# The first unit's output product: its second half as three products of split numbers, and a new order of the parts

## The chip, the cores and the metric

The kernel runs on one core of one Trainium2 chip. The metric is the device time of one execution in microseconds (us); the median of several runs is taken. TensorE is called PE here (PEld is its loading of weights), VectorE DVE, ScalarE ACT, GpSimd POOL, and SyncE, which issues the DMAs, SP.

## What is computed

Local attention over chunks of 32 tokens, then a channel mix ("ch" below stands for one chunk's queries and the keys and values in its reach, with 8 memory tokens):

```
a   = softmax(scale * q_ch @ k_ch.T);  x = a @ v_ch        # B=4, H=8, S=768, D=64
xk  = mu_k * x + (1 - mu_k) * x_prev;  xr = mu_r * x + (1 - mu_r) * x_prev
k   = max(xk @ w_k, 0)                                     # 512 -> 1024
v   = (k * k) @ w_v                                        # 1024 -> 512
out = sigmoid(xr @ w_r) * v
```

The weights arrive as 64-bit floats and become fp32 on the chip; the result is fp32.

## The kernel before

**Units.** The 4 x 768 tokens are cut into 12 units of 256 tokens (`UTOK`), each of two blocks of 128 tokens (c = 0, 1). Each unit goes through scores (named s in the order below), transposes of the softmax (t, one for each block), the product with v (a, one for each block, giving x), the hidden layer (h, four parts, each with 256 of the 1024 hidden columns), the gate (g, one for each block), and the output product (v, or p from unit 2 on).

**Two ways to multiply.** An fp32 product takes fp32 operands as they are. The split way writes each number as a high part and a low part of the type fp32r (`kh`, `kl` for the squared activations, `wv_hl` for w_v, `xh`, `xl` for the mixed inputs) and makes three products in place of one: high x high, high x low, low x high. Unit 0 is done in fp32 all through (`is_whole`, line 383), unit 1 by split products, and units from `FAST` = 2 on by a scheme of seven split products (`products`, line 743).

**The output product of units 0 and 1** (lines 1099 to 1157). For each block c there are two parts of the inner sum over 1024: half 0 uses the hidden columns of f = 0 and 1, half 1 those of f = 2 and 3. So its parts are named v0.0.0 (unit 0, block 0, half 0), v0.0.1, v0.1.0 and v0.1.1. Both halves of a block accumulate in one bank of PSUM (`pv`). In unit 0 a part is four fp32 products of 128 x 512 (line 1112), each of which stands in the trace as two records; in unit 1 it is twelve split products (line 1124). When a block's two parts are done, DVE multiplies with the sigmoid of the gate (`f_o`, line 1145) and SP stores it.

**Preparing the operands.** ACT applies relu and square to the hidden layer (lines 1047, 1054); for split products ACT or DVE then writes `kh` (line 1060) and DVE `kl` (line 1072). Each of the ten weight pieces (four of w_k, two of w_r, four of w_v) is loaded as 64-bit words, joined to fp32 on ACT and DVE (lines 325 to 332), and later split: the high part by ACT or DVE (line 335, shown under the copying helper, lines 271 and 273), the low part by DVE (line 345). The low parts of w_v go to buffers in which raw pieces of w_v lay (`lows`, line 300), two pieces to a buffer. For units after the first, the mixed input is made by a difference (`df`, line 607), a mixing (line 617), a high part and a low part (`xl`, line 633).

**Storage order.** The columns of w_v and w_r are put by the host into two halves (even columns first). Split products read the moving operand "woven" (`woven`, line 50: one word from each half in turn), which puts the result back into natural order. Unit 0's fp32 products read it straight, and the final multiply undoes the order (line 1149).

**What sets the order.** Every operation is given to a planner (`Plan`, line 81) with a cost, the operations that it waits for, and its buffers. PE's order is written out by hand for the start (`LEAD`, line 34) and continued by `te_order` (line 186); the first 230 planned operations (`STRICT`) keep PE strictly in that order. Operations of the other engines have no order of their own: each gets a due time, counted back from those that need it, and the planner gives every engine the operation that can start first, with a preference for the earlier due time (line 166). Each engine, and SP's queue of DMAs, then runs its list strictly in turn.

Of the kernel before, what the change touches and what calls it, by code (L numbers as in the profile page):

```python
# [16 lines left out]
P = 128  # L17
# [3 lines left out]
DM, DFF = 512, 1024  # L21
# [3 lines left out]
KT = DM // P  # L25
# [2 lines left out]
NEG = -3.0e38  # L28
TINY = 2.0**-112
LOOK = 400  # L30
STRICT = 230
EASE = 0.1
TURNS = 3
LEAD = "s0.0 s0.1 t0 a0 t1 a1 h0.0.0 h0.0.1 s1.0 h0.1.0 h0.2.0 s1.1 h0.3.0 h0.3.1 h0.3.2 h0.3.3 g0.0 g0.1 t2 t3 v0.0.0 a2 a3 v0.0.1 s2.0 v0.1.0 v0.1.1 h1.0 h1.1 t4 t5 h1.2 a4 a5 h1.3 g1.0 g1.1"
UTOK = 256
FAST = 2
ROWS = [(0, 0, 1), (0, 1, 1), (1, 0, 2), (2, 0, 2), (3, 0, 2)]
# [19 lines left out]
def pairs(a):  # L57
    return a.rearrange("p (n t) -> p n t", t=2)
# [127 lines left out]
def te_order():  # L186

    nu = B * S // UTOK
    seq = [tuple([x[0]] + [int(n) for n in x[1:].split(".")]) for x in LEAD.split()]
    for u in range(1, nu):  # L190
        a, b = 2 * u + 2, 2 * u + 3
        g = [("g", u + 1, c) for c in range(QPU)]
        h = [("h", u, f) for f in range(FT // 2)]
        v = [("v", u, c, n) for c in range(QPU) for n in range(2)]
        n = 1 if u == nu - 2 else 2
        seq += h[:n] + [("t", a), ("t", b)] + h[n : n + 1] + [("a", a), ("a", b)] + h[n + 1 :]
        if u >= FAST:
            v = [("p", u, n) for n in (1, 7, 6, 4, 5, 2, 3)]
            if u >= nu - 2:
                g = [("g", nu - 1, u - (nu - 2))]  # L200
            if u == nu - 1:
                v = v[:5] + [("p", u, 2, 0), ("p", u, 3), ("p", u, 2, 1)]
            seq += v[:2] + [("s", u + 2, 0)] + g + v[2:]
            continue
        seq += v[:1] + [("s", u + 2, 0)] + g + v[1:]
    seq = list(dict.fromkeys(seq))
    last = {"t": B * NQT, "a": B * NQT}
    seq = [x for x in seq if x[1] < last.get(x[0], nu)]
    due, t = {}, 6.0
    for x in seq:  # L210
        assert x not in due
        due[x] = t
        t += PE_COST[x[0]] * (0.66 if x[:3] == ("h", 0, 0) else 0.33 if x[:3] == ("h", 0, KT - 1) else 1.32 if x[:2] == ("h", 0) else 1.32 if x[1] == 0 and x[0] in "gv" else 1)
    return due


# [1 line left out]
def local_attention__then__channel_mix(  # L218
# [56 lines left out]
    def either(late=False, **alts):  # L275
        return [(n, *alts[n]) for n in alts if n != "pool"]
# [103 lines left out]
    def word_deps(hl, ks):  # L380
        return [whole[id(hl[0]), k][0] for k in ks], [whole[id(hl[0]), k][1] for k in ks]

    def is_whole(u, part):
        return u == 0

    xdone = {}
    xslot, pslot = {}, {}
# [547 lines left out]
    def channel_mix(u):  # L935
        b, t0 = units[u]

        def f_gate(c):
            p = T["pr", u, c] = ps("m", f"pr{u}_{c}")
            if is_whole(u, "g"):  # L940
                for k in range(KT):
                    w = T["w", id(wr_hl[0]), k // 2][:, k % 2 * DM : (k % 2 + 1) * DM]
                    nc.tensor.matmul(  # L943
                        p, T["xf", u, 1][:, k, c * P : (c + 1) * P], w, start=(k == 0), stop=(k == KT - 1)
                    )
                return
            xh, xl = T["xh", u, 1], T["xl", u, 1]
            wh, wl = ([w[k // 2][:, k % 2 * DM : (k % 2 + 1) * DM] for k in range(KT)] for w in wr_hl)
            for k in range(KT):
                for n, (x, w) in enumerate(((xh, wh[k]), (xh, wl[k]), (xl, wh[k]))):  # L950
                    nc.tensor.matmul(  # L951
                        pairs(p), x[:, k, c * P : (c + 1) * P], woven(w),
                        start=(k + n == 0), stop=(k == KT - 1 and n == 2),
                    )

        def f_sig(c):
            if c == 0:
                T["sg", u] = sb("sg", [P, QPU * DM], f"sg{u}")
            p, sg = T["pr", u, c], T["sg", u][:, c * DM : (c + 1) * DM]
            if is_whole(u, "v") and not is_whole(u, "g"):  # L960
                p = p.rearrange("p (n t) -> p t n", t=2)
                sg = sg.rearrange("p (t n) -> p t n", t=2)
            nc.scalar.activation(sg, p, AF.Sigmoid)  # L963

        wr, wr_use = wdeps(wr_hl, range(KT // 2)), []
        if is_whole(u, "g"):
            wr, wr_use = word_deps(wr_hl, range(KT // 2))
        sgs = Slot("sg")
        gs = [Slot("m") for _ in range(QPU)]
# [1 line left out]
        for c in range(QPU):  # L971
            grp.append(
                op(
                    ("pe", FULL if is_whole(u, "g") else BLOCK), lambda c=c: f_gate(c),
                    grp[-1:] + (list(mix[u, 1][0].values()) if is_whole(u, "g") else list(mix[u, 1][:2])) + wr,
                    new=[gs[c]], use=list(mix[u, 1][2:]) + wr_use, due=due["g", u, c],
                )
            )
# [41 lines left out]
        for f in range(FT // 2):  # L1020
# [39 lines left out]
                copy(e, h, part())  # L1060

            kl = Slot("st") if f == 0 else Slot("kh4") if f == 1 else Slot("kf0") if f == 2 else kl

            def f_lo(e, f=f, part=part, kl=kl):
                if f < 2:
                    l = sb(kl.tag, [P, 2, UTOK], f"kl{u}_{f}", F32R)
                else:
                    if f == 2:
                        T["kl", u] = sb(kl.tag, [P, 4, UTOK], f"kl{u}_{f}", F32R)
                    l = T["kl", u][:, 2 * f - 4 : 2 * f - 2]  # L1070
                T["kl", u, f] = l
                e.tensor_sub(l, part(), T["kh", u, f].bitcast(F32))
# [10 lines left out]
            )  # L1083
            relu = oa
            ob = op(either(act=(0.54,), dve=(0.62, True)), f_sq, [oa], use=[kf])
            if is_whole(u, "v") or u >= FAST:
                ks.append((ob, None, kf, kf))
                continue
            o2 = op(either(act=(0.54,), dve=(0.35, True)), f_hi, [ob], new=[kh], use=[kf])
            o3 = op(  # L1090
                either(dve=(0.62, True)), f_lo, [o2] + ([o3] if f == 3 else []),
                new=[kl] * (f < 3), use=[kf, kh] + [kl] * (f == 3),
            )
            ks.append((o2, o3, kh, kl))

# [3 lines left out]
        for c in range(QPU):  # L1099
            s = Slot("m")  # L1100
            prev = None
            for half in range(2):
                fs = range(FT // 4 * half, FT // 4 * (half + 1))

                def f_s2(c=c, half=half, fs=fs):
                    if half == 0:
                        T["pv", u, c] = ps("m", f"pv{u}_{c}")
                    p = T["pv", u, c]
                    if is_whole(u, "v"):
                        for f in [2 * f2 + i for f2 in fs for i in range(2)]:  # L1110
                            w = T["w", id(wv_hl[0]), f // 2][:, f % 2 * DM : (f % 2 + 1) * DM]
                            nc.tensor.matmul(  # L1112
                                p, T["kf", u, f // 4][:, f % 4, c * P : (c + 1) * P], w, start=(f == 0), stop=(f == FT - 1)
                            )
                        return
                    wh, wl = ([w[f // 2][:, f % 2 * DM : (f % 2 + 1) * DM] for f in range(FT)] for w in wv_hl)
                    for f2 in fs:
                        for i in range(2):
                            f = 2 * f2 + i
                            kh = T["kh", u, f2][:, i]  # L1120
                            kl = T["kl", u, f2][:, i]
                            tc_ = slice(c * P, (c + 1) * P)
                            for n, (x, w) in enumerate(((kh, wh[f]), (kh, wl[f]), (kl, wh[f]))):
                                nc.tensor.matmul(  # L1124
                                    pairs(p), x[:, tc_], woven(w), start=(f + n == 0), stop=(f == FT - 1 and n == 2)
                                )

                deps, use = [prev], []
                for f in fs:
                    deps += ks[f][:2]  # L1130
                    use += ks[f][2:]
                if is_whole(u, "v"):
                    wd, wd_use = word_deps(wv_hl, fs)
                    deps += wd
                    use += wd_use
                else:
                    deps += wdeps(wv_hl, fs)
                dv = due["v", u, c, half]
                prev = op(("pe", FULL if is_whole(u, "v") else BLOCK), f_s2, deps, new=[s] if half == 0 else [], use=use + ([s] if half else []), due=dv)
                if u == 0:  # L1140
                    first_v.append(prev)
                if u == FAST - 1:
                    last_v.append(prev)

            def f_o(c=c):
                o = T["o", u, c] = sb("o", [P, DM], f"o{u}_{c}")
                p, sg = T["pv", u, c], T["sg", u][:, c * DM : (c + 1) * DM]
                if is_whole(u, "v"):
                    o, p, sg = pairs(o), woven(p), woven(sg)
                nc.vector.tensor_mul(o, p, sg)  # L1150

            def f_st(c=c):
# [81 lines left out]
```

## Time and profile before

| | us |
|---|---|
| Median of 3 runs | 389.33 (388.58 to 390.25) |
| The profiled execution | 389.12 |
| Its span in the profile | 387.3 |
| PE busy | 381.1 (98%) |
| DVE busy | 317.7 (82%) |
| ACT busy | 219.6 (57%) |
| Output product of unit 0, line 1112 (32 records) | 14.4 busy |
| Output product of unit 1, line 1124 (48 records) | 18.3 busy |

The granted clock of PE is 1.0 throughout. The span runs from the first to the last instruction on the chip; the profiled execution's own time has some 2 us more around it. A group of PE instructions shows each record's time from its start to its modelled end; neighbours overlap, so the time that a stage takes on PE is read from the chain or from the starts in the timeline. In a line of the timeline stand start, duration, engine, line, operation, output and inputs, the shapes, and how many such instructions were merged.

### The profile page before, as it was taken

How to read it: one execution, taken by the hardware profiler on the slowest of the kernel's cores; microseconds unless marked ns; L12 is line 12 of the kernel's file. 1: busy time of each engine (PE TensorE's matmuls, PEld its weight loads, DVE VectorE, ACT ScalarE, POOL GpSimd, SP SyncE). 2: the span in 40 equal slices, each digit the busy share in tenths (PEclk: the TensorE clock that was granted, in tenths of full speed). 3: DMA queues.
4: the chain of work that ended last, by engine and by line, in shares of the span. 5: the costliest groups of instructions: out<-in, count | busy, mean ns of one | idle time of the engine just before them, and what ended most of it. 6: DMA issues, size and time to landing. Idle time of an engine off the chain costs nothing.

```text
span 387.3 us, 10714 instructions
## 1 busy us (share of the span) xinstructions
PE 381.1 (98%) x4768; PEld 350.8 (91%) x4768; DVE 317.7 (82%) x509; ACT 219.6 (57%) x326; POOL 2.8 (1%) x13
## 2 busy tenths in 40 slices
PE   8899999999999999999999999999999999999996
PEld 6786559988999999999999999999999999999996
DVE  2998999998799699699699689789779869969264
ACT  1797985763645564464465366267267356567260
POOL 2000000000000000000000000000000000000000
PEclk9999999999999999999999999999999999999999
DMA  8999882320052143134134134134134120000101
GB/s 313 418 397 396 312 287 89 110 83 27 30 193 84 52 155 121 54 122 155 54 113 164 57 110 164 56 110 164 56 110 164 57 90 22 30 29 2 54 2 54
DMA packets 13053, 48.98 MB, mean 126 GB/s; under 512 B 1488, under 2 KB 1872, under 8 KB 12496
## 3 DMA queue, kind: packets, MB, share of 16 engines
q1 hardware_dynamic: 13008, 48.31, 33.4%
q8 instruction: 37, 0.61, 0.7%
q14 instruction: 8, 0.07, 0.1%
HBM read 42.01 MB, written 6.29 MB: 125 GB/s over the span
## 4 chain that ended last, share of the span: by engine, by line
PE 97%; DVE 1%; issue 0%; ACT 0%; DVEq 0%
PE ph L1028 31%; PE pr L951 15%; PE accy L856 10%; PE accz L856 7%; PE accx L856 7%; PE px L526 6%; PE s L429 4%; PE ph L1000 4%; PE pv L1112 4%; PE pt L509 3%; PE pv L1124 3%; PE pr L943 2%; PE warm L1180 2%; DVE mx L442 0%; DVE e L447 0%
## 5 line engine op out<-in xcount | busy, mean ns | idle before, releaser
L1028 PE MATMUL ph<-xh,wk 128*128 128x256 f32 x352 | 99.0, 281 | 0.0
L1028 PE MATMUL ph<-xl,wk 128*128 128x256 f32 x352 | 96.8, 275 | 0.0
L1028 PE MATMUL ph<-xh,wl 128*128 128x256 f32 x352 | 96.8, 275 | 0.0
L1047 ACT ACTIVATE kf<-ph 128x512 f32<-128x512 f32 x47 | 27.9, 598 | 73.8 <-PE ph L1028 73.7
L1028 PEld LDWEIGHTS ph<-xh,wk 128*128 128x128 f32 x352 | 67.5, 192 | 0.9 <-issue 0.2
L1028 PEld LDWEIGHTS ph<-xl,wk 128*128 128x128 f32 x352 | 67.6, 192 | 0.3 <-issue 0.2
L1028 PEld LDWEIGHTS ph<-xh,wl 128*128 128x128 f32 x352 | 67.6, 192 | 0.0
L273 DVE COPY aTz<-pt 64x512 f32<-64x512 f32 x20 | 13.9, 694 | 27.5 <-PE pt L509 18.0
L951 PE MATMUL pr<-wr,xh 128*128 128x512 f32 x88 | 34.3, 390 | 0.0
L801 DVE TENSOR_TENSOR al<-kf,ah 128x512 fp32r<-128x512 f32 x50 | 33.5, 686 | 0.5
L951 PE MATMUL pr<-wr,xl 128*128 128x512 f32 x88 | 33.4, 379 | 0.0
L951 PE MATMUL pr<-wl,xh 128*128 128x512 f32 x88 | 33.4, 379 | 0.0
L453 ACT ACTIVATE e<-e 128x1024 f32<-128x1024 f32 (+1 forms) x13 | 12.9, 992 | 34.7 <-DVE e L447 34.6
L526 PEld LDWEIGHTS px<-aTz,vw 128*64 128x64 f32 x768 | 23.5, 138 | 3.8 <-issue 1.8
L526 PE MATMUL px<-aTz,vw 128*64 128x64 f32 x768 | 25.2, 224 | 1.1 <-issue 1.1
L1054 ACT ACTIVATE kf<-kf 128x512 f32<-128x512 f32 x40 | 25.3, 633 | 1.3 <-DVE kf L1049 0.4
L271 ACT CAST ah<-kf 128x512 fp32r<-128x512 f32 x40 | 24.9, 622 | 1.8 <-DVE kf L779 1.2
L271 ACT CAST xh<-df 128x1024 fp32r<-128x1024 f32 x11 | 16.3, 1482 | 12.2 <-DVE df L617 12.2
L856 PE MATMUL accx<-wl,ah 128*128 128x256 f32 x80 | 22.0, 275 | 0.0
L856 PE MATMUL accx<-wv,al 128*128 128x256 f32 x80 | 22.0, 275 | 0.0
L856 PE MATMUL accx<-wv,ah 128*128 128x256 f32 x80 | 22.0, 275 | 0.0
L963 ACT ACTIVATE sg<-pr 128x512 f32<-128x512 f32 x24 | 14.3, 604 | 10.3 <-PE pr L951 10.3
(124 smaller groups left out, 937.2 us busy)
## 6 DMA issues: line engine op xcount, KB each, us to landing
qk<-in_qk_dram SPq DMA_DIRECT2D x24, 768.0 KB, 6.2
vw<-in_vw_dram SPq DMA_DIRECT2D x24, 512.0 KB, 4.6
out_dram<-o SPq DMA_DIRECT2D x23, 256.0 KB, 2.0
raw<-in_w_k_dram SPq DMA_DIRECT2D x4, 1024.0 KB, 12.5
raw<-in_w_v_dram SPq DMA_DIRECT2D x4, 1024.0 KB, 9.4
raw<-in_w_r_dram SPq DMA_DIRECT2D x2, 1024.0 KB, 8.0
out_dram<-o SPq DMA_DIRECT2D x2, 128.0 KB, 1.7
id_sb<-in_ident_dram SPq DMA_DIRECT2D x1, 64.0 KB, 5.5
```

The source lines that it names most:

```text
L271: e.copy(dst, src)
L429: nc.tensor.matmul(s5[CHUNK * j : CHUNK * (j + 1), h, d - c, r, :], q4[z, r, j, :], k4[z, r, j, :], start=True, stop=True,)
L526: nc.tensor.matmul(p3[64 * h : 64 * h + 64, 2 * g : 2 * g + 2, CHUNK * j : CHUNK * j + CHUNK], v[:, g, h, j, :], a[:, h, g, j, :], start=True,
L801: nc.vector.tensor_sub(low(n), place[n](), T["ah", u, n].bitcast(F32))
L856: nc.tensor.matmul(o, x, w, start=(n in fresh and c + i == 0), stop=(c == cs[-1] and i == 2), skip_group_check=True)
L951: nc.tensor.matmul(pairs(p), x[:, k, c * P : (c + 1) * P], woven(w), start=(k + n == 0), stop=(k == KT - 1 and n == 2),)
L963: nc.scalar.activation(sg, p, AF.Sigmoid)
L1000: nc.tensor.matmul(p[:, i * UTOK + c * P : i * UTOK + (c + n) * P], T["w", id(wk_hl[0]), k][:, fc], T["xf", u, 0][:, k, z], start=(i + k + ...
L1028: nc.tensor.matmul(pairs(p[:, i * UTOK : (i + 1) * UTOK]), w[:, fc], x[:, :, k].rearrange("p t n -> p n t"), start=(k + n == 0), stop=(k = ...
L1047: e.activation(part(), p, AF.Relu)
L1054: e.activation(q, q, AF.Square)
L1112: nc.tensor.matmul(p, T["kf", u, f // 4][:, f % 4, c * P : (c + 1) * P], w, start=(f == 0), stop=(f == FT - 1))
```

## The change

1. `is_whole` takes the half of the inner sum: unit 0's gate and hidden layer and half 0 of its output product stay fp32; half 1 (v0.0.1 and v0.1.1) is made by three split products, for which `kh` and `kl` of f = 2 and 3 are made for unit 0 too, and pieces 2 and 3 of w_v must be split by then.
2. So that both halves fit in one bank of PSUM, the fp32 products of gate and output read w woven, too; the sigmoid and the final multiply no longer reorder.
3. `kl` of unit 0 gets buffers of its own (`sl`, `sm6`), which the seven-product scheme uses later.
4. The hand-written order: v0.1.0 comes before v0.0.1; t4, t5, a4 and a5 come after all of h1.0 to h1.3 (t4 and t5 ahead of g1.0, a4 and a5 between g1.0 and g1.1); v1.0.0 and s3.0 are now part of the list. `STRICT` goes to 260. The due times count v's half 1 as a split product.

```diff
-STRICT = 230
+STRICT = 260
-LEAD = "... g0.0 g0.1 t2 t3 v0.0.0 a2 a3 v0.0.1 s2.0 v0.1.0 v0.1.1 h1.0 h1.1 t4 t5 h1.2 a4 a5 h1.3 g1.0 g1.1"
+LEAD = "... g0.0 g0.1 t2 t3 v0.0.0 a2 a3 v0.1.0 s2.0 v0.0.1 v0.1.1 h1.0 h1.1 h1.2 h1.3 t4 t5 g1.0 a4 a5 g1.1 v1.0.0 s3.0"
...
-    def is_whole(u, part):
-        return u == 0
+    def is_whole(u, half=0):
+        return u == 0 and half == 0
...
                     nc.tensor.matmul(
-                        p, T["xf", u, 1][:, k, c * P : (c + 1) * P], w, start=(k == 0), stop=(k == KT - 1)
+                        pairs(p), T["xf", u, 1][:, k, c * P : (c + 1) * P], woven(w),
+                        start=(k == 0), stop=(k == KT - 1),
                     )
...
             kl = Slot("st") if f == 0 else Slot("kh4") if f == 1 else Slot("kf0") if f == 2 else kl
+            if u == 0:
+                kl = Slot(("sl", "sm6")[f % 2])
...
-            if is_whole(u, "v") or u >= FAST:
+            if is_whole(u, z) or u >= FAST:
                 ks.append((ob, None, kf, kf))
                 continue
...
-                    if is_whole(u, "v"):
+                    if is_whole(u, half):
...
                             nc.tensor.matmul(
-                                p, T["kf", u, f // 4][:, f % 4, c * P : (c + 1) * P], w, start=(f == 0), stop=(f == FT - 1)
+                                pairs(p), T["kf", u, f // 4][:, f % 4, c * P : (c + 1) * P], woven(w),
+                                start=(f == 0), stop=False,
                             )
...
-                if is_whole(u, "v"):
-                    o, p, sg = pairs(o), woven(p), woven(sg)
                 nc.vector.tensor_mul(o, p, sg)
```

More of the change, by code (lines that the diff above doesn't have):

```diff
@@ L30 @@
 LOOK = 400
-STRICT = 230
+STRICT = 260
 EASE = 0.1
 TURNS = 3
-LEAD = "s0.0 s0.1 t0 a0 t1 a1 h0.0.0 h0.0.1 s1.0 h0.1.0 h0.2.0 s1.1 h0.3.0 h0.3.1 h0.3.2 h0.3.3 g0.0 g0.1 t2 t3 v0.0.0 a2 a3 v0.0.1 s2.0 v0.1.0 v0.1.1 h1.0 h1.1 t4 t5 h1.2 a4 a5 h1.3 g1.0 g1.1"
+LEAD = "s0.0 s0.1 t0 a0 t1 a1 h0.0.0 h0.0.1 s1.0 h0.1.0 h0.2.0 s1.1 h0.3.0 h0.3.1 h0.3.2 h0.3.3 g0.0 g0.1 t2 t3 v0.0.0 a2 a3 v0.1.0 s2.0 v0.0.1 v0.1.1 h1.0 h1.1 h1.2 h1.3 t4 t5 g1.0 a4 a5 g1.1 v1.0.0 s3.0"
 UTOK = 256
@@ L212, in te_order @@
         due[x] = t
-        t += PE_COST[x[0]] * (0.66 if x[:3] == ("h", 0, 0) else 0.33 if x[:3] == ("h", 0, KT - 1) else 1.32 if x[:2] == ("h", 0) else 1.32 if x[1] == 0 and x[0] in "gv" else 1)
+        t += PE_COST[x[0]] * (0.66 if x[:3] == ("h", 0, 0) else 0.33 if x[:3] == ("h", 0, KT - 1) else 1.32 if x[:2] == ("h", 0) else 1.32 if x[1] == 0 and x[0] in "gv" and (x[0], x[-1]) != ("v", 1) else 1)
     return due
@@ L939, in f_gate @@
             p = T["pr", u, c] = ps("m", f"pr{u}_{c}")
-            if is_whole(u, "g"):
+            if is_whole(u):
                 for k in range(KT):
@@ L959, in f_sig @@
             p, sg = T["pr", u, c], T["sg", u][:, c * DM : (c + 1) * DM]
-            if is_whole(u, "v") and not is_whole(u, "g"):
-                p = p.rearrange("p (n t) -> p t n", t=2)
-                sg = sg.rearrange("p (t n) -> p t n", t=2)
             nc.scalar.activation(sg, p, AF.Sigmoid)
         wr, wr_use = wdeps(wr_hl, range(KT // 2)), []
-        if is_whole(u, "g"):
+        if is_whole(u):
             wr, wr_use = word_deps(wr_hl, range(KT // 2))
@@ L973, in channel_mix @@
                 op(
-                    ("pe", FULL if is_whole(u, "g") else BLOCK), lambda c=c: f_gate(c),
-                    grp[-1:] + (list(mix[u, 1][0].values()) if is_whole(u, "g") else list(mix[u, 1][:2])) + wr,
+                    ("pe", FULL if is_whole(u) else BLOCK), lambda c=c: f_gate(c),
+                    grp[-1:] + (list(mix[u, 1][0].values()) if is_whole(u) else list(mix[u, 1][:2])) + wr,
                     new=[gs[c]], use=list(mix[u, 1][2:]) + wr_use, due=due["g", u, c],
@@ L1062, in channel_mix @@
             kl = Slot("st") if f == 0 else Slot("kh4") if f == 1 else Slot("kf0") if f == 2 else kl
+            if u == 0:
+                kl = Slot(("sl", "sm6")[f % 2])
             def f_lo(e, f=f, part=part, kl=kl):
-                if f < 2:
+                if f < 2 or u == 0:
                     l = sb(kl.tag, [P, 2, UTOK], f"kl{u}_{f}", F32R)
@@ L1090, in channel_mix @@
             o3 = op(
-                either(dve=(0.62, True)), f_lo, [o2] + ([o3] if f == 3 else []),
-                new=[kl] * (f < 3), use=[kf, kh] + [kl] * (f == 3),
+                either(dve=(0.62, True)), f_lo, [o2] + ([o3] if f == 3 and u else []),
+                new=[kl] * (f < 3 or u == 0), use=[kf, kh] + [kl] * (f == 3 and u > 0),
             )
@@ L1112, in f_s2 @@
                             nc.tensor.matmul(
-                                p, T["kf", u, f // 4][:, f % 4, c * P : (c + 1) * P], w, start=(f == 0), stop=(f == FT - 1)
+                                pairs(p), T["kf", u, f // 4][:, f % 4, c * P : (c + 1) * P], woven(w),
+                                start=(f == 0), stop=False,
                             )
                         return
-                    wh, wl = ([w[f // 2][:, f % 2 * DM : (f % 2 + 1) * DM] for f in range(FT)] for w in wv_hl)
                     for f2 in fs:
@@ L1119, in f_s2 @@
                             f = 2 * f2 + i
+                            wh, wl = (w[f2][:, i * DM : (i + 1) * DM] for w in wv_hl)
                             kh = T["kh", u, f2][:, i]
@@ L1122, in f_s2 @@
                             tc_ = slice(c * P, (c + 1) * P)
-                            for n, (x, w) in enumerate(((kh, wh[f]), (kh, wl[f]), (kl, wh[f]))):
+                            for n, (x, w) in enumerate(((kh, wh), (kh, wl), (kl, wh))):
                                 nc.tensor.matmul(
@@ L1131, in channel_mix @@
                     use += ks[f][2:]
-                if is_whole(u, "v"):
+                if is_whole(u, half):
                     wd, wd_use = word_deps(wv_hl, fs)
@@ L1138, in channel_mix @@
                 dv = due["v", u, c, half]
-                prev = op(("pe", FULL if is_whole(u, "v") else BLOCK), f_s2, deps, new=[s] if half == 0 else [], use=use + ([s] if half else []), due=dv)
+                prev = op(("pe", FULL if is_whole(u, half) else BLOCK), f_s2, deps, new=[s] if half == 0 else [], use=use + ([s] if half else []), due=dv)
                 if u == 0:
@@ L1147, in f_o @@
                 p, sg = T["pv", u, c], T["sg", u][:, c * DM : (c + 1) * DM]
-                if is_whole(u, "v"):
-                    o, p, sg = pairs(o), woven(p), woven(sg)
                 nc.vector.tensor_mul(o, p, sg)
```

## The prediction, made before the result was known

> **What bounds the kernel now.** I read the page first: its span, the busy shares and the engines of the chain that ended last; then who kept PE (TensorE) waiting.
>
> ```profile
> span 387.3 us, 10714 instructions
> PE 381.1 (98%) x4768; PEld 350.8 (91%) x4768; DVE 317.7 (82%) x509; ACT 219.6 (57%) x326; POOL 2.8 (1%) x13
> PE 97%; DVE 1%; issue 0%; ACT 0%; DVEq 0%
> ```
>
> ```profile
> PE warm L1180 <- DVE zero_sb L260: 1.2, 1, 1.2
> PE px L526 <- issue: 1.1, 2, 0.6
> ```
>
> PE is busy for 98% of the span, the chain lies on it for 97%, and its longest waits (1.2 us at the very start, 1.1 us in two pieces) are over before the stage that the change touches. So the kernel is bound by what is issued to PE. Time leaves it when PE's list gets shorter, and comes back as soon as PE has to wait. The busy column of PE alone wouldn't prove this, since matmul ends are modelled; the chain does, where one piece starts when the piece before it ends. I therefore read the chain in order of time, from the first product with w_v on (start us, us, what):
>
> ```profile
> 41.78 3.44 PE pv L1112 x8
> ...
> 47.23 3.63 PE pv L1112 x8
> ...
> 52.28 7.06 PE pv L1112 x16
> 59.34 5.36 PE ph L1028 x48
> 64.70 0.87 PE pt L509 x8
> ...
> 68.25 2.02 PE px L526 x64
> ...
> 73.14 5.18 PE pr L951 x24
> 78.32 2.59 PE pv L1124 x12
> 80.91 1.41 PE s L429 x89
> 82.33 5.38 PE pr L951 x24
> ```
>
> The first unit's output parts are 41.78 (v0.0.0), 47.23 (v0.0.1) and 52.28 (v0.1.0 and v0.1.1 together), in fp32. Unit 1 does the same sum by split products (L1124). 52.28 + 7.06 = 59.34, so there is no hole ahead of h1.0; and so on to 82.33. To this belong the instructions by form:
>
> ```profile
> L1112 PE MATMUL pv<-w,kf 128*128 128x512 f32 x32 | 14.4, 599 | 0.0
> ...
> L1124 PE MATMUL pv<-wv,kh 128*128 128x512 f32 x16 | 6.1, 379 | 0.0
> ```
>
> **What PE saves.** One part (one 128-token block, half of the inner sum) has four blocks of the sum. The fp32 form shows two records for each, 8 a part: 3.44 us, or 0.43 us a record. (The 599 ns of the group is an instruction from start to modelled end; the ends overlap, so it is not what PE pays.) The split form has three products for each block, 12 a part: 2.59 us, 0.216 us each. The change turns two parts (v0.0.1, v0.1.1) from the first form into the second: 2 x 3.44 - 2 x 2.59 = 1.70 us less on PE. The 0.19 us by which the second part (3.63) exceeds the first follows the small matmuls that stand ahead of it; 82.33 shows the same 0.2 behind the scores for split products (5.38 against 5.18), so it stays, wherever the parts are put.
>
> The load of weights is the one thing here that could spoil this:
>
> ```profile
> L1112 PEld LDWEIGHTS pv<-w,kf 128*128 128x128 f32 x32 | 5.8, 190 | 6.4 <-issue 6.2
> ...
> L1124 PEld LDWEIGHTS pv<-wv,kh 128*128 128x128 f32 x16 | 3.0, 189 | 0.4
> ```
>
> ```profile
> 78.16 0.38 PE L1124 MATMUL pv<-wv,kh 128*128 128x512 f32 x1
> 78.38 0.38 PE L1124 MATMUL pv<-wl,kh 128*128 128x512 f32 x1
> ```
>
> Loads go from 8 to 12 a part, at 189 ns each. The products start 0.22 us apart although a load of 0.19 us lies between them, so the load runs beside the product before it. The Trainium skill (TensorE: Matmul & The Clock Gate, Part 3, What overlaps and what doesn't) says that a load overlaps running matmuls only when it targets another row group. These loads use all 128 rows, so by that rule they would not overlap; the trace, with 0.22 us from start to start, does not agree.
>
> **The form of the remaining fp32 products.** The gate of unit 0 (16 records) and its remaining fp32 halves (16) now read their moving operand "woven", alternating between the two halves of the row, and write in order; the trace has no fp32 product of that kind. The nearest row is L1124, which reads woven words of the same four bytes at 0.216 us for 512, twice as fast as an fp32 record. A reader that delivers that rate is not the limit of a record that takes 0.43 us. I take zero. The bounds: each record takes twice as long (32 x 0.43 = +13.8 us), or they come down to 0.216 us (-6.8 us). The sigmoid and the final multiply move as many elements as before: zero.
>
> **What the other engines get.** The low and high halves of w_v and of the squared activations are now wanted at v0.0.1, not first at unit 1. Rows of DVE around that time, then one of ACT:
>
> ```profile
> 45.08 1.23 DVE L332 SCALAR_TENSOR_TENSOR w<-w,raw 128x1024 uint32<-128x1024 uint32 x1
> 46.22 2.48 DVE L345 TENSOR_TENSOR wl<-w,wk 128x1024 fp32r<-128x1024 f32 x2
> 48.61 1.22 DVE L607 TENSOR_TENSOR df<-xT 128x1024 f32<-128x1024 f32 x1
> 49.87 1.67 DVE L617 SCALAR_TENSOR_TENSOR xf<-df,mu_sb,xT 128x256 f32<-128x256 f32 x4
> 51.57 0.70 DVE L1150 TENSOR_TENSOR o<-pv,sg 128x512 f32<-128x512 f32 x1
> 52.19 1.22 DVE L345 TENSOR_TENSOR wl<-w,wk 128x1024 fp32r<-128x1024 f32 x1
> ...
> 53.64 1.23 DVE L442 TENSOR_REDUCE mx<-s 128x16 f32<-128x1024 f32 x1
> 54.78 1.22 DVE L633 TENSOR_TENSOR xl<-xf,xh 128x1024 fp32r<-128x1024 f32 x1
> 55.91 1.22 DVE L447 TENSOR_TENSOR e<-s,mx 128x1024 f32<-128x1024 f32 x1
> ...
> 64.20 1.22 DVE L345 TENSOR_TENSOR wl<-w,wr 128x1024 fp32r<-128x1024 f32 x1
> ...
> 68.25 0.69 DVE L1072 TENSOR_TENSOR kl<-kf,kh 128x512 fp32r<-128x512 f32 x1
> 68.85 1.22 DVE L345 TENSOR_TENSOR wl<-w,wv 128x1024 fp32r<-128x1024 f32 x1
> ...
> 76.91 1.67 DVE L617 SCALAR_TENSOR_TENSOR df<-df,mu_sb,xT 128x256 f32<-128x256 f32 x4
> ...
> 79.28 1.23 DVE L633 TENSOR_TENSOR xl<-xf,xh 128x1024 fp32r<-128x1024 f32 x1
> ```
>
> ```profile
> 48.98 2.00 ACT L271 CAST wv<-w 128x1024 fp32r<-128x1024 f32 x2
> ...
> 63.35 0.64 ACT L271 CAST kh<-kf 128x512 fp32r<-128x512 f32 x1
> ```
>
> DVE starts its next instruction 0.1 us before the record of the last one ends: a subtraction of 1024 costs it 1.14 (54.78 to 55.91), one of 512 0.60 (68.25 to 68.85). Two kl are new (1.2 us); two wl of w_v move forward from after 67 us to before 52 us (2.28 us). DVE thus has 3.48 us more to do ahead of unit 1, and no hole to put it in; PE meanwhile arrives 1.70 us earlier. I go through PE's deadlines, carrying the order of DVE of before along:
>
> *v0.0.1, now at 52.28* (v0.1.0 has taken its place ahead of the scores). The join of the last w_v piece ends by 46.2 (both wl wait for it: their tile reuses its load buffer). Two wl and two kl behind it end at 46.2 + 3.48 = 49.7. One wk subtraction may still stand ahead of them: 50.8. ACT must put the casts of pieces 2 and 3 of w_v (1.0 us each) where it casts others at 48.98, and add two kh (0.64 each) once the squares are there. Cost zero, 1.5 us of cover; without that cover each instruction more ahead of it would cost 1.14.
>
> *h1.0, at 59.34 - 1.70 = 57.64.* It needs xl, which ended at 54.78 + 1.22 = 56.0. With 3.48 more ahead of it, less the 0.62 of the output multiply of 51.57 (its part now ends only near 55), it would end at 58.9: 1.2 us of stall. But the maximum of the scores at 53.64 (with its memset about 1.25 us) need not stand ahead of it. The planner ranks by due time, counted back from the first reader on PE, and t4 moves behind all four h1 parts, from 64.70 to 57.64 + 4 x 2.68 = 68.36 (5.36 for two parts). So xl falls due first and ends at 57.6. Stall between 0 and 1.2; I take 0.2, since the rank favours xl.
>
> *g1.0, at 68.36 + 0.87 = 69.23.* The last it needs is the second wl of w_r, which ended at 64.20 + 1.22 = 65.4; plus 3.48 gives 68.9. Zero, with 0.3 us of cover. The transposes t4 and t5 need the softmax that stood ahead of that row, and come no earlier than 68.36.
>
> *g2.0.* PE runs g1.0, a4 and a5, g1.1, v1.0.0 and the scores from 69.23 (2.59 + 2.02 + 2.59 + 0.2 + 2.59 + 1.41): 80.63, where it was 82.33. It needs the xl that ended at 79.28 + 1.23 = 80.5. The two wl are done either way before it, so only the 1.2 of the kl is added: 81.7; less the mixing of the other operand at 76.91 (1.6), due only at h2.0: 80.1. Its input chain starts later too: a5 ends at 73.84, and a copy to xT (about 0.6 as an estimate from the 512-wide rows), one df (1.14), one mix (1.6), a cast (0.7, as an estimate from the kl row) and xl (1.14) end at 79.0. Cover 0.5 us; I take zero.
>
> **What moves on the queues.** The output multiply and store of block 0 come some 4 us later. On SP's queue the next two loads of q and k stand behind that store, and the loads of vw for t6 and t7 wait for the later a4 and a5:
>
> ```profile
> 52.74 1.95 SPq L404 DMA_DIRECT2D qk<-in_qk_dram  x2
> ...
> 69.37 1.26 SPq L503 DMA_DIRECT2D vw<-in_vw_dram  x2
> ```
>
> Even 4 us later the first are issued more than 20 us ahead of the scores that follow v1.0.0, and the second come 3 to 4 us later, with unit 2 still to start. POOL has nothing in this stage. Zero.
>
> **The sum.** The profiled execution took 389.12 us: 387.3 of span and 1.8 around it. 389.12 - 1.70 + 0.2 = 387.6. The median of the three runs (389.33) lies 0.2 above the profiled one, so on that scale I say 387.8 us.
>
> **Rivals.**
>
> *DVE piles up ahead of h1.0 (20%).* If DVE keeps the maximum and the subtraction of the scores (53.64 and 55.91, 1.25 + 1.14) ahead of xl, as it is free to do once v0.0.1 is served, xl ends at 57.6 + 2.4 = 60.0 and h1.0 stalls by 2.4: slower by 0.7, 390.0 us. Should the multiply be kept in front as well (0.6), it is 390.6. It decides from the point where the stall at h1.0 passes 1.70 us. For it: DVE has no hole. Against it: the due times, and that xl is ready for it.
>
> ```profile
> 52.30:59.30 7.00, 7.00 (x18) 3.17 (x19) 6.88 (x10) 5.23 (x6) 0.00 (x0) 1.00 0.81 290
> ```
>
> Here (PE, PEld, DVE, ACT, POOL, then the granted clock) DVE is busy 6.88 of 7.00 us, ACT 5.23. The clock of PE is 1.00, as there is no hole. The Trainium skill (TensorE: Matmul & The Clock Gate, Part 1) states that an idle window of about 3.4 us halves that clock; no run shown here has such a hole, and 2.4 us would be shorter.
>
> *The gain is lost in small waits further on (6%).* g1.0 and g2.0 have 0.3 and 0.5 us of cover. If each misses by one 1024-wide instruction (1.14), the waits are 0.8 and 0.6; with the 0.2, gain is 0.1: 389.2.
>
> *The woven fp32 products run at another rate (5%).* +13.8 - 1.7 would be 401.4, -6.8 - 1.7 would be 380.8. For either speaks only that no row shows them.
>
> *Loads do not hide (2%).* Then a record of a part costs its stream and its load: 16 x (0.43 + 0.19) against 24 x (0.216 + 0.189), 9.9 against 9.7: a gain of 0.2, 389.1. The starts at 78.16 and 78.38 speak against it.
>
> **How the numbers follow.** My forecast, stalls from 0 to 0.8 us and so a gain of 0.9 to 1.7, has 67%: 387.6 to 388.4. The range must leave out no more than 2 in 10: below, the full 1.70 and the spread of a median (the three runs span 388.58 to 390.25) take it to 386.8; above, the first rival takes it to 390.1. A difference of 0.5%, about 1.95 us, is what a measurement of this kernel can tell from no change; the full saving on PE (1.70 us, 0.44%) is just below it. So faster by over 0.5% comes from the forecast only when no stall at all meets a favourable measurement (three tenths of it, 0.20) and from the faster half of the woven case (0.02) and chance order on DVE and ACT elsewhere (0.02): 0.24. Slower by over 0.5% needs a stall over 3.6 us, a quarter of the first rival (0.05), and the slower half of the woven case (0.03): 0.08. The rest, 0.68, is no change that can be told.
>
> **What would show it.** Right: pv L1112 falls to 16 records, two split parts of 2.59 us appear behind s2.0, h1.0 starts at 57.6 to 57.9, g1.0 near 69.3, g2.0 near 80.7, from there on each piece of PE's chain is 1.5 us earlier, and the gate still takes 6.9 us for 16 records. Wrong on the stall: PE idle ahead of h1.0 with xl or wl of w_k as releaser (first rival), or ahead of g1.0 or g2.0 (second). Wrong on the rate: a gate record far from 0.43. It would also be wrong if waits of PE beyond 125 us, where the change touches nothing, came or went.

## The result, and the profile after

The changed kernel takes 390.95 us (median of 7 runs, 390.65 to 391.51), the kernel before 388.85 (median of 7): a ratio of 1.005, 95% interval 1.0035 to 1.0066. That is slower by 2.1 us by the medians (1.4 to 2.6 by the interval), where a gain of 1.5 was forecast, and above the stated range of 386.8 to 390.1. The page of the profile after, first the span and the busy shares, then who kept PE waiting:

```profile
span 388.5 us, 10736 instructions
...
PE 382.2 (98%) x4776; PEld 351.8 (91%) x4776; DVE 319.1 (82%) x510; ACT 221.4 (57%) x329; POOL 2.8 (1%) x13
```

```profile
PE warm L1179 <- DVE zero_sb L260: 1.2, 1, 1.2
PE px L526 <- issue: 1.1, 2, 0.6
PE s L429 <- issue: 0.3, 1, 0.3
PE pt L509 <- DVE e L463: 0.2, 1, 0.2
```

No new wait of PE: the kernel before has the same four waits, of the same length. The 2.1 us are therefore in PE's own list, and the chain in order of time (start us, us, what) shows in which piece:

```profile
17.21 3.78 PE ph L998 x32
...
33.32 8.64 PE pr L943 x16
...
42.83 4.32 PE pv L1112 x8
...
49.16 4.51 PE pv L1112 x8
...
55.09 5.38 PE pv L1125 x24
60.47 10.72 PE ph L1026 x96
...
72.06 2.59 PE pr L952 x12
...
83.45 5.38 PE pr L952 x24
...
96.60 5.36 PE ph L1026 x48
```

The same chain of the kernel before, where it wasn't shown yet:

```profile
17.94 3.77 PE ph L1000 x32
...
34.04 6.87 PE pr L943 x16
...
95.47 5.36 PE ph L1028 x48
```

The gate of unit 0, still fp32 with 16 records, went from 6.87 to 8.64 us; a first half of 8 records from 3.44 to 4.32. Both are 0.540 us a record in place of 0.430. The two split parts (55.09) take 5.38, as forecast. The start-up of a profiled execution varies by up to 1 us (the first hidden product starts between 17.14 and 18.11 in the profiles of all runs here), so stages are best compared from the first hidden product to h2.0: 95.47 - 17.94 = 77.53 before, 96.60 - 17.21 = 79.39 after, +1.86. The parts add up: 32 records x 0.110 = +3.53, less the 1.70 saved, = +1.83. From h2.0 to the end both have the same left, 387.3 - 95.47 = 291.8 and 388.5 - 96.60 = 291.9. In the groups by form, kernel after and then kernel before, the slower record shows too, in the mean:

```profile
L1112 PE MATMUL pv<-w,kf 128*128 128x512 f32 x16 | 9.1, 709 | 0.0
L943 PE MATMUL pr<-w,xf 128*128 128x512 f32 x16 | 8.8, 703 | 0.0
```

```profile
L943 PE MATMUL pr<-w,xf 128*128 128x512 f32 x16 | 7.0, 592 | 0.0
```

599 and 592 ns became 709 and 703: 0.11 us for each record, in the gate and in the output product alike.

### The profile page after: what moved, and what is told of

It is laid out like the page before. It is cut to its first block, busy times and chain, and to the rows that moved or that the text cites. A ratio compares the mean times of both kernels' runs of the same rounds, so it can differ in the third digit from the quotient of the medians.

```text
span 388.5 us, 10736 instructions
## 1 busy us (share of the span) xinstructions
PE 382.2 (98%) x4776; PEld 351.8 (91%) x4776; DVE 319.1 (82%) x510; ACT 221.4 (57%) x329; POOL 2.8 (1%) x13
## 4 chain that ended last, share of the span: by engine, by line
PE 97%; DVE 1%; issue 0%; ACT 0%; DVEq 0%
PE ph L1026 31%; PE pr L952 15%; PE accy L856 10%; PE accz L856 7%; PE accx L856 7%; PE px L526 6%; PE s L429 4%; PE pv L1125 4%; PE ph L998 4%; PE pt L509 3%; PE pv L1112 2%; PE pr L943 2%; PE warm L1179 1%; DVE mx L442 0%; DVE e L447 0%
## 5 line engine op out<-in xcount | busy, mean ns | idle before, releaser
L273 DVE COPY aTz<-pt 64x512 f32<-64x512 f32 x20 | 13.8, 692 | 28.3 <-PE pt L509 19.1
```

## The experiments

My theory after the result (W): reading the moving operand woven costs an fp32 record a quarter of its time. Rivals: the order or the write in PSUM (P), other traffic at that time (T), the new order of the parts (O).

**Straight read, spread write.** The changed kernel, with the weave moved from the read to the write:

```diff
-pairs(p), T["xf", u, 1][:, k, c * P : (c + 1) * P], woven(w),
+p.rearrange("p (n t) -> p t n", t=2), T["xf", u, 1][:, k, c * P : (c + 1) * P], w.rearrange("p (t n) -> p t n", t=2),
...
-pairs(p), T["kf", u, f // 4][:, f % 4, c * P : (c + 1) * P], woven(w),
+p.rearrange("p (n t) -> p t n", t=2), T["kf", u, f // 4][:, f % 4, c * P : (c + 1) * P], w.rearrange("p (t n) -> p t n", t=2),
```

> The changed kernel, but unit 0's fp32 products (16 records of the gate, 16 of the first halves) read w straight and write the result spread over the bank (every second word), so the order in PSUM stays natural. Theory W (reading the moving operand woven costs an fp32 record 0.11 us, 0.54 in place of 0.43): both groups return to 0.43 us a record, PE's list is 32 x 0.11 = 3.5 us shorter, and the time falls from 391.0 to about 387.4. Rival P (it is the order of the columns in PSUM, or the write, that costs): stays at 0.54 and 391.0, or comes out slower still. Rival T (other traffic in 33 to 54 us slows PE there): stays at 0.54. For the stalls on DVE: with h1.0 some 3.5 us earlier, near 57, xl (which ended at 57.9 in the changed kernel) may now be late; 0 to 1.2 us of waiting there.

387.68 us against 388.92 of the kernel before, ratio 0.9967 (0.9954 to 0.998). The chain:

```profile
17.20 3.77 PE ph L998 x32
...
33.30 6.87 PE pr L943 x16
...
41.04 3.44 PE pv L1112 x8
...
46.49 3.63 PE pv L1112 x8
...
51.53 5.38 PE pv L1125 x24
56.91 10.72 PE ph L1026 x96
67.62 0.87 PE pt L509 x8
68.50 2.59 PE pr L952 x12
...
93.04 5.36 PE ph L1026 x48
```

Both groups are back at 0.43; T falls, and so does P: the columns lie in PSUM in the same order as in the changed kernel, and the write is now the spread one. From 17.20 to 93.04 are 75.84 us, 1.69 less than before: the saving on PE in full. The medians of the whole time differ by 1.24 us, 0.8 to 1.8 by the interval of the ratio. It beats both kernels. This run also tests the forecast of DVE's deadlines, as h1.0 comes as early as it was reckoned. From DVE's timeline:

```profile
54.61 1.53 DVE L633 TENSOR_TENSOR xl<-xf,xh 128x1024 fp32r<-128x1024 f32 x1
...
58.70 1.23 DVE L442 TENSOR_REDUCE mx<-s 128x16 f32<-128x1024 f32 x1
...
67.84 1.22 DVE L345 TENSOR_TENSOR wl<-w,wr 128x1024 fp32r<-128x1024 f32 x1
...
78.26 1.23 DVE L633 TENSOR_TENSOR xl<-xf,xh 128x1024 fp32r<-128x1024 f32 x1
```

xl ends at 56.1, ahead of h1.0 (56.91), and the maximum of the scores stands behind it, not in front. The second low half of w_r ends at 69.1, 0.6 after the start of g1.0, and costs nothing: it belongs to the second half of the inner sum, which g1.0 reaches 1.3 us after its start.

**Everything of unit 0 straight,** its 24 split products too:

```diff
-pairs(p), T["xf", u, 1][:, k, c * P : (c + 1) * P], woven(w),
+p, T["xf", u, 1][:, k, c * P : (c + 1) * P], w,
...
-pairs(p), T["kf", u, f // 4][:, f % 4, c * P : (c + 1) * P], woven(w),
+p, T["kf", u, f // 4][:, f % 4, c * P : (c + 1) * P], w,
...
-pairs(p), x[:, tc_], woven(w), start=(f + n == 0), stop=(f == FT - 1 and n == 2)
+pairs(p) if u else p, x[:, tc_], woven(w) if u else w,
+start=(f + n == 0), stop=(f == FT - 1 and n == 2)
...
+if u == 0:
+    o, p, sg = pairs(o), woven(p), woven(sg)
 nc.vector.tensor_mul(o, p, sg)
```

> The changed kernel, but everything of unit 0 that reads w_v or w_r reads it straight, the 24 split products of its second halves too; the final multiply undoes the order as in the kernel before. Theory W: the fp32 records return to 0.43 us. For the 24 split products the two theories differ: if the weave costs only fp32 and does nothing for fp32r, they stay at 0.216 us and the time is that of the first kernel, about 387.4; if fp32r is the type that gains from the weave (as every split product in the kernel uses it), straight ones take longer, say 0.27 to 0.43 us, and 1.3 to 5 us of the saving goes.

388.06 us, ratio 0.9975 (0.9966 to 0.9984). The fp32 groups are at 6.87 and 3.44 us again, but

```profile
52.14 5.80 PE pv L1125 x24
```

the split products take 0.42 us more than woven (5.38). Without the 0.2 us at the start that is 0.233 us each against 0.216. So fp32r gains from the weave by which fp32 loses, but by less than expected (0.27 to 0.43 us straight, 1.3 to 5 us in all).

**The woven gate alone,** put into the kernel before:

```diff
-p, T["xf", u, 1][:, k, c * P : (c + 1) * P], w, start=(k == 0), stop=(k == KT - 1)
+pairs(p), T["xf", u, 1][:, k, c * P : (c + 1) * P], woven(w), start=(k == 0), stop=(k == KT - 1)
...
-o, p, sg = pairs(o), woven(p), woven(sg)
+o, p, sg = pairs(o), woven(p), pairs(sg)
```

> The kernel before with one part of the change alone: unit 0's gate reads w_r woven (16 records); its output product stays fp32 and straight. Theory W: the gate takes 8.6 us in place of 6.9, the output product stays at 0.43 us a record, the time rises by 1.8 us, to 390.6 with the kernel before at 388.9. Rivals P and T: T says no change at all (order and traffic are those of the kernel before), P the same as W.

391.07 us, ratio 1.005 (1.0037 to 1.0063), 1.9 us by the ratio. The gate alone went up, by 1.77 us, and the output product, still straight, did not. The order of the parts, the split products and the write (in order, one word beside the next) are as in the kernel before here, so the read alone is left as the cause:

```profile
33.24 8.64 PE pr L943 x16
...
42.75 3.43 PE pv L1112 x8
```

**The new order alone,** in the kernel before: only `LEAD` and `STRICT`.

```diff
-STRICT = 230
+STRICT = 260
-LEAD = "... v0.0.0 a2 a3 v0.0.1 s2.0 v0.1.0 v0.1.1 h1.0 h1.1 t4 t5 h1.2 a4 a5 h1.3 g1.0 g1.1"
+LEAD = "... v0.0.0 a2 a3 v0.1.0 s2.0 v0.0.1 v0.1.1 h1.0 h1.1 h1.2 h1.3 t4 t5 g1.0 a4 a5 g1.1 v1.0.0 s3.0"
```

> The kernel before with the new hand-written order and STRICT = 260 alone; all arithmetic as before. If the order is free (theory W): within 0.3 us of the kernel before, 388.9, no waits of PE. Rival O (the order costs, through DVE or the later transposes): slower by 1 to 3 us, with PE waiting ahead of g1.0 or g2.0.

388.8 us, ratio 0.9999 (0.999 to 1.0008); 77.53 us from the first hidden product (18.10) to h2.0 (95.63), as before. O falls: the order by itself is free, to within the 0.4 us of the interval.

**The weave on other fp32 products.** The first experiment, with unit 0's hidden layer reading its mixed input woven where it has 256 columns:

```diff
+weave = woven if n == 2 else lambda a: a
...
-p[:, i * UTOK + c * P : i * UTOK + (c + n) * P], T["w", id(wk_hl[0]), k][:, fc],
-T["xf", u, 0][:, k, z],
+weave(p[:, i * UTOK + c * P : i * UTOK + (c + n) * P]), T["w", id(wk_hl[0]), k][:, fc],
+weave(T["xf", u, 0][:, k, z]),
```

> The first run (straight read, spread write for gate and first halves), and besides unit 0's hidden layer with 256 columns (48 fp32 records) reads the mixed input woven over 128 words and writes spread, so the result is in its place. A dose of the weave on other fp32 products: if it costs a quarter of the record, 0.222 becomes 0.28 and the 10.75 us of these 48 records become 13.4, the kernel 2.7 us slower than the first run (about 390.4); if the cost is 0.11 us a record whatever its width, 5.3 us; if it needs rows of 512 or w as operand, nothing.

The pieces with 256 columns, in the first experiment and then in this run:

```profile
21.75 7.10 PE ph L998 x32
...
29.65 3.65 PE ph L998 x16
```

```profile
22.66 8.94 PE ph L999 x32
...
32.39 4.56 PE ph L999 x16
```

7.10 + 3.65 = 10.75 us became 13.50: +2.75, 0.057 for 256 columns where 512 cost 0.110. So the cost goes with the columns and is not special to w. The write is spread here too, which cost nothing at 512 columns in the first experiment. One run took 390.75, with the kernel before at 389.07.

**Which orders of reading are slow?** Five runs with other orders, the gate and the first halves in fp32, the two split parts in fp32r, each 512 words with the write contiguous; they leave out putting the columns of unit 0's output back in place. In place of `woven(w)` stands, in the changed kernel, one of these (with `m`, `s` and `n` as named):

```diff
-woven(w)
+w.rearrange("p (t n m) -> p n t m", t=2, m=2)
+w.rearrange("p (n s) -> p s n", s=2)
+w.rearrange("p (b e n) -> p b n e", e=2, n=32)
```

The first reads pairs (quads with m=4), the second with a step of s, the third woven over n words. Pairs and steps of 2:

> The changed kernel with other orders of reading w in unit 0, the write contiguous, so that the columns of unit 0's output are in a wrong order (left out: putting them right). The gate (16 fp32 records) and v0.0.1 (12 split products) read pairs: two neighbouring words from one half, two from the other. The first halves (16 fp32 records) and v0.1.1 (12 split products) read with a step of 2: all even words, then all odd ones. Theory N (an fp32 record is fast as long as words come in neighbouring pairs): gate at 0.43 us a record, first halves at 0.54. Theory J (it is the jump between two far places that costs): gate between 0.43 and 0.54 as it jumps half as often, first halves at 0.43. For fp32r, which took 0.242 straight and 0.224 woven (with the 0.2 us of the first one spread over 24): if the reverse of N holds, pairs 0.23 to 0.24 and step 2 0.216; if jumps help, pairs 0.22 and step 2 0.235.

```profile
33.98 7.25 PE pr L943 x16
...
42.11 3.60 PE pv L1112 x8
...
52.93 9.57 PE pv L1125 x24
```

Pairs 0.453, step 2 0.450: both cost 0.02 over the straight read. N (single words cost 0.11, neighbouring pairs nothing) falls with step 2, which reads single words and is no slower than pairs. The split products took 0.33 and 0.45, where 0.216 to 0.24 was expected. Weaves over 32 and 2 words:

> As the run before, with weaves over shorter distances (columns of unit 0's output again in a wrong order). The gate and v0.0.1 alternate between words 32 apart, the first halves and v0.1.1 between words 2 apart. Theory N: both fp32 groups at 0.54 us, no matter how far. Theory J: 32 apart near 0.54 or less, 2 apart near 0.43, as both words then lie within 16 bytes. For fp32r: 0.216 in both if any weave helps.

```profile
34.13 8.58 PE pr L943 x16
...
43.59 3.44 PE pv L1112 x8
...
54.08 5.60 PE pv L1125 x24
```

0.536 and 0.430; the split products woven over 2 words took 0.236, as slow as straight ones, where 0.216 was expected. Weaves over 8 and 4:

> As the run with weaves over 32 and 2 words, now 8 words in the gate and v0.0.1, 4 words in the first halves and v0.1.1 (columns of unit 0's output again in a wrong order). At 32 words an fp32 record took 0.536 us, at 2 words 0.43; split products 0.216 and 0.236. If the border is a block of 16 words (64 bytes): 8 apart stays within one block as 2 apart does, both fp32 groups 0.43, split products 0.236. If it is 8 words (32 bytes): the gate 0.54, the first halves 0.43. If it is 4 words: both 0.54, split products 0.216.

```profile
33.74 8.57 PE pr L943 x16
...
43.19 4.34 PE pv L1112 x8
...
55.49 5.38 PE pv L1125 x24
```

0.536 and 0.543, and the split products back at 0.216, so for both types the border lies between 2 and 4 words. Weaves over 2 and over 4 words both change place at every word and differ in the distance alone, so changing place at every word isn't what costs. 16 words:

> The gate and v0.0.1 woven over 16 words, v0.1.1 over 4, the first halves with a step of 2 as in the earlier run (a repeat: 0.45 us a record). If the border is a block of 16 words (64 bytes): gate 0.54 (two blocks), v0.0.1 0.216. If the border lies at 32 words: gate 0.43, v0.0.1 0.236.

The gate took 8.74 us, 0.546 a record, and the repeat of step 2 0.450. Last, steps of 4 and quads:

> Two more orders of reading (columns of unit 0's output in a wrong order): the gate and v0.0.1 with a step of 4, the first halves and v0.1.1 in quads, four neighbouring words from one half, then four from the other. So far an fp32 record took 0.43 us straight and woven over 2, 0.45 in pairs and with step 2, 0.54 woven over 4, 8, 16, 32 or 256. Theory K (what counts is how many words running come from one block of four words, 16 bytes): step 4 takes one from each block, so 0.54; quads take four, so 0.43, though they jump to the other half as a weave does. Rival J (the jump between far places costs): step 4 near 0.45 as step 2, quads between 0.43 and 0.45.

```profile
33.48 14.40 PE pr L943 x16
...
48.76 3.43 PE pv L1112 x8
...
59.25 8.75 PE pv L1125 x24
```

Quads 0.429: free, though they jump 256 words after every fourth word, so J (the jump) falls. Step 4 took 0.90, not the 0.54 of K, so K is right on which orders are slow, and not on how slow. The single runs of these five, in the order told, took 392.68, 389.91, 391.03, 389.49 and 398.2 us, the kernel before 389.04 to 389.07. All together, us for 512 words in one fp32 record or one split product (fp32r from the starts of its products in the timeline). Most of the other orders were read in one execution only, and that a block of four starts at every fourth word is supposed, not seen:

| words running from one block of four | order | fp32 | fp32r |
|---|---|---|---|
| 4 | straight | 0.43 | 0.23 |
| 4, in another order | weave over 2 | 0.43 | 0.236 |
| 4 | quads | 0.43 | 0.25 |
| 2 | pairs | 0.45 | 0.33 |
| 2 | step 2 | 0.45 | 0.45 |
| 1, and back to the block at once | weave over 4, 8, 16, 32, 256 | 0.54 to 0.55 | 0.216 |
| 1, never back | step 4 | 0.90 | 0.46 |

**The old order with the split halves.** The first experiment with `LEAD` and `STRICT` of the kernel before.

```diff
-STRICT = 260
+STRICT = 230
-LEAD = "... v0.0.0 a2 a3 v0.1.0 s2.0 v0.0.1 v0.1.1 h1.0 h1.1 h1.2 h1.3 t4 t5 g1.0 a4 a5 g1.1 v1.0.0 s3.0"
+LEAD = "... v0.0.0 a2 a3 v0.0.1 s2.0 v0.1.0 v0.1.1 h1.0 h1.1 t4 t5 h1.2 a4 a5 h1.3 g1.0 g1.1"
```

> The first run (split second halves, straight read, spread write) with the hand-written order and STRICT of the kernel before: v0.0.1 follows a3 at once, so it is wanted at 46.5 in place of 51.5. In the first run DVE finished the low halves for it at 47.1 and 48.8 (w_v) and 47.7 and 49.4 (kl). Theory D (DVE's deadlines are as worked out in the prediction, so the new order is what gives cover): PE waits some 1.3 us ahead of v0.0.1 and little after; of the 1.24 us that the first run gained 0 to 0.4 stay: 388.5 to 389.2 with the kernel before at 388.9. Rival: the planner gets the low halves ready earlier or the order doesn't matter: no wait, 387.7.

389.53 us, ratio 1.0016 (1.0006 to 1.0025): no gain is left, and a bit more is gone than theory D put. Who kept PE waiting, the two products of v0.0.1 that waited longest, and two pieces of the chain, which runs over DVE from 41 to 65 us:

```profile
PE pt L509 <- DVE e L463: 1.1, 2, 0.9
```

```profile
48.24 0.48 PE L1125 MATMUL pv<-wv,kl 128*128 128x512 f32 x1
...
49.98 0.48 PE L1125 MATMUL pv<-wv,kl 128*128 128x512 f32 x1
```

```profile
54.73 1.23 DVE mx L442
...
57.09 1.44 DVE xl L633
```

v0.0.1 (47.33 to 51.04 in the timeline, 3.7 us) took some 0.9 us more than its 2.79 because its kl and wl came as it ran (the two kl ended at 48.19 and 49.93 in DVE's timeline); D had put 1.3. What D had not put is t4: it waits 0.9 us for the softmax of unit 2. Here the maximum of the scores does stand ahead of xl, as the first rival feared, because t4 stands between h1.1 and h1.2 and makes it due by the planner's reckoning. Even so xl ended at 58.54 and h1.0 started at 58.58, where the part before it ended, so h1.0 itself did not stall. So the order that was free in the kernel before is what pays for the split halves.

## Why the prediction was wrong

- *What bounds the kernel* held: a product that took longer, with no engine waiting, went into the time almost one to one (+1.83 on PE, +2.1 us by the medians).
- *What PE saves* held: 1.70 us reckoned, 1.69 in the run with the straight read.
- ***The form of the remaining fp32 products* failed.** It said "A reader that delivers that rate is not the limit of a record that takes 0.43 us. I take zero." The rate was taken from woven fp32r products. Measured: +0.110 us a record, 3.53 us for 32, twice the saving. The step treated the read as one limit and the array as another, the larger of the two counting; the runs show that the type and the order of reading act together, and that the two types even go opposite ways on the same words. The bounds held it (-6.8 to +13.8), but the case got 5%, and only its ends were priced. Its nearest row wasn't of the same type, and no row of the type in question with another order existed; that calls for a larger chance. With 3.53 us for this term and no stall, the prediction's own sum gives 387.8 - 0.2 + 3.53 = 391.1 us; 390.95 was measured.
- *The other engines* held: no new wait of PE in the changed kernel, nor with the straight read. There h1.0, g1.0 and g2.0 start at 56.91, 68.50 and 79.90; with the 0.74 us by which that profile started earlier they are 57.65, 69.24 and 80.64, where 57.6 to 57.9, 69.3 and 80.7 were forecast. The stall at h1.0 put at 0.2 was 0, since the planner put xl first, as reckoned from the due times. At g1.0 the cover of 0.3 was not there (the low half of w_r ended 0.6 after its start), but the prediction had asked for it too early: the second half of the sum is its first reader. At g2.0 xl ended at 79.5 with PE there at 79.90: a cover of 0.4, reckoned as 0.5.
- *The queues* cost nothing, as put: no wait of PE on a DMA stands in the profiles after and with the straight read.
- *The rivals*: DVE ahead of h1.0 did not come; the order on DVE that it feared appears only with the old order of the parts, and the wait there falls on t4. Small waits further on did not come either. Loads stayed hidden (5.38 us for 24 products). The third, another rate for woven fp32, was the one that happened.

The Trainium skill (Advanced Engine Details and Errata, SBUF Cachelines) states that SBUF is read in lines of 16 bytes and that at least two accesses in a row must fall on one line to absorb the latency. The trace agrees for fp32: four words 0.43, two 0.45, one 0.54 or 0.90. It doesn't agree for fp32r, which is fastest woven (0.216), with one word from each line. The rule on PSUM of the same page of the Trainium skill (Advanced Engine Details and Errata, PSUM Cachelines: consecutive elements should lie side by side, or matmuls slow down much) isn't borne out for fp32 records: the spread write of the first experiment cost nothing (6.87 us for 16 records, the same as contiguous). For fp32r no run here shows it.

What stays open: why fp32r gains where fp32 loses, and why step 4 costs fp32 0.47 us where the weave costs 0.11. That lines of 16 bytes are behind it fits which orders are slow for fp32, but not how slow step 4 is; it was inferred from the times, not seen.

## What to carry to other kernels

When a change makes one product share a bank with another, look at how its operands are now read, not only at how many products there are: a reordering by which one type gains can cost another a quarter. Put the reordering where it is free; here that was the write into PSUM, which turned 390.95 into 387.68 us. A saving on the bound engine is worth what the engine next to it can follow: the split halves gained only together with the order that gave DVE another 5 us for them (v0.0.1 at 51.53 us in place of some 46.5).

## What the runs showed of the hardware that was not expected

The same 512 words take an fp32 record 0.43 to 0.90 us, and a split product 0.216 to 0.46, by the order of the read alone; the best order of the one (straight) isn't that of the other (weave over 4 words or more). And the ten matmuls that warm up PE at the very start took 4.64 us in the profile before, 4.07 in the profile after, and from 3.98 to 4.64 over all runs, from the same instructions, so spans of single profiles differ by up to 0.7 us for no reason that the change gives.
